# Windowed attention and a gated unit on one core: the gate's convolution in sixteen parts of the array, an added zero block, and a frozen order

## The chip, the core and the metric

The kernel runs on one core of a Trainium2 chip. The metric is the device time of one execution in microseconds. A core has five engines with a queue each: TensorE (PE, matrix products; its weight loads are shown apart as PEld), VectorE (DVE), ScalarE (ACT), GpSimd (POOL) and SyncE (SP, which here issues all transfers). Products go to PSUM, and DVE and ACT bring them back to SBUF.

## What is computed

Eight batches of 576 tokens, eight heads of 64. Heads 0 to 3 ("plain") look at the last 32 tokens, heads 4 to 7 ("dilated") at every fourth of the last 128. The attention result x, 512 wide, goes through a gated unit:

```python
scores = scale * np.matmul(q, k.transpose(0, 1, 3, 2))
mask_plain = (rel >= 0) & (rel < window)                    # window 32
mask_dil = (rel >= 0) & (rel < window * dilation) & (rel % dilation == 0)
attn = softmax(np.where(mask, scores, -1e9)); x = attn @ v
for k in range(K):                                          # K = 5, per channel
    gate_pre += conv_w[k][None, None, :] * xp[:, k:k + S, :]
gate = 1.0 / (1.0 + np.exp(-gate_pre))
val = x @ w_val
return (gate * val @ w_out)
```

## The kernel before

**Attention.** q and k come as fp32 into eight `qk` tiles; PE transposes their upper halves (read as bf16) into PSUM, and ACT or DVE copies them to `qT` and `kT`. Plain heads do this in groups of 18 transposes (`plain`, L581), dilated heads in groups of five (`dilated`, L647): four of 128 rows and one of the 64 rows that remain of 576. For each pair of heads, `attend` runs two score groups of six products (L513), exp on ACT (L520), the mask on DVE (L527), twelve products with v (L536), and the normalization on DVE (L545, L546). x is transposed back (L610 plain, L673 dilated) into `xT`, which holds 512 channels as four chunks of 128 partitions, for two batches side by side.

**The gated unit** (`gated`) works on two batches as three blocks of 384 tokens, the last two batches as four blocks of 288: 13 blocks. A block takes its four chunks in two pairs. For a pair the convolution (L716) is five taps of matmuls with a 64x64 diagonal matrix of the tap's weights as stationary operand, so a pair is 20 matmuls on 64x64 parts of the array, 26 groups in all. Then tanh on ACT (L727), the projection (L735, eight matmuls), and gate times value on DVE into `yT` (L745). In odd chunks the two halves of the channels change places in the convolution's output, and the weights are arranged to match. Last come 36 output tiles of 128 tokens (`outputs`: L765, copied out by L772 or L774, stored by L778).

**PSUM and buffers.** Three double tiles `pd` (two banks each; scores, products with v, plain transposes, convolution, projection) and two single tiles `pu` (dilated transposes, x transposes, outputs).

**What sets the order.** Each piece is a `Task` with the engines that may run it and estimated durations. `Plan.run` (L235) is a list scheduler: it keeps a clock for each engine, models the transfers and TensorE's clock, and at each step emits the task with the earliest start and best priority; the numbers in `TUNE` shift the priorities. It also inserts warm matmuls on a constant tile where it expects PE to wait (`emit`, L848 to L851). Each engine's queue runs in the order of emission. On SP at most five large loads are under way (`depth`), and a store waits in the same queue for its tile.

**Start.** `early` sets constants: the identity, masks, and the constant columns of the buffers. `weights` loads the convolution's weights (three small transfers, first in SP's queue now), builds `conv_diag`, loads `w_val` and `w_out` and casts them on POOL (w_val in 16 pieces of 64 columns, to set the channels in order).

Of the kernel before, what the change touches and what calls it, by code (L numbers as in the profile page):

```python
# [10 lines left out]
BF16 = mybir.dt.bfloat16  # L11
# [6 lines left out]
TUNE = {'seed': 918663,  # L18
 'jit': 0.211,
 'lag': 3.109,  # L20
 'plain': 0.758,
 'unit': -1.097,
 'half': -2.425,
 'chunk': 0.105,
 'look': {'PE': 0, 'ACT': 0.088, 'DVE': 0.03, 'POOL': 0.029, 'SP': 1.597},
 'flex': 0.555,
 'switch': 0.116,
 'conv': -3.876,
 'wv': 2.184,
 'wo': 0.85,  # L30
 'bufs': {'ps2': 3,
          'ps1': 2,
          'qk': 8,
          'vp': 2,
          'vd': 2,
          'vn': 2,
          'qT': 4,
          'kT': 4,
          'et': 5,
          'xn': 4,  # L40
          'gate': 3,
          'osb': 5,
          'xT': 3,
          'yT': 3,
          'vw': 2,
          'wt': 3},
 'kind': {'G': 1.939,
          'Xd': 1.011,
          'Ad': 0.718,
          'Sp': -5.15,  # L50
          'Tqp': 4.695,
          'Ap': 5.165,
          'Ekd': -5.633,
          'Eqd': 1.426,
          'ST': 2.599,
          'Y': -6.337,
          'Ed': -3.471,
          'Wv': -13.219,
          'Lqd': 0.336,
          'C': 0.77,  # L60
          'Lqp': 0.22,
          'Tqd': -0.449,
          'Lvp': 0.647,
          'Fp': 5.651,
          'U': 9.706,
          'H': 2.869,
          'Ep': -5.164,
          'Md': 1.158,
          'Ct': -1.059,
          'Xp': -1.728,  # L70
          'Tkd': 5.919,
          'Fd': -1.349,
          'Nd': -2.418,
          'Lc': -2.674,
          'Lwo': 2.488,
          'Sd': -3.39,
          'Wo': -6.282,
          'early': -0.684,
          'EO': 5.987,
          'Cd': 7.203,  # L80
          'Ekp': -10.843,
          'Tkp': -11.573,
          'Np': 3.065,
          'Lvd': 0.594,
          'Eqp': -4.056,
          'Lkr': -0.08,
          'Lkp': -0.622,
          'Mp': -3.736,
          'Lqr': -0.16,
          'Lwv': -0.381,  # L90
          'Lkd': 0.451,
          'V': 2.925,
          'O': 8.299,
          'HD': 8.634,
          'HA': -5.829,
          'HC': 11.348,
          'HB': 9.605,
          'Lvf': -0.397},
 'depth': 5,
 'heat': 6,  # L100
 'page0': 440,
 'lookq': 4.0,
 'nat': 4}
# [8 lines left out]
class Ten:  # L112


    def __init__(self, cls):
        self.cls = cls
        self.idx = None
        self.left = 0
        self.end = 0.0


class Task:
    def __init__(self, name, eng, fn, deps=(), tens=(), prio=0.0, mode=None, xfer=0.0, n=1, act=0.0, out=None):
# [5 lines left out]
        self.prio = prio  # L129
        self.mode = mode  # L130
        self.xfer = xfer
        self.n = n
        self.act = act
        self.out = out
        self.on = None
        self.load = False
        self.end = None
        self.users = []
        self.missing = len(self.deps)
        for d in self.deps:  # L140
            d.users.append(self)
        for t in self.tens:
            t.left += 1


class Plan:


    LAT = {PE: 0.22, ACT: 0.17, DVE: 0.17, POOL: 0.18, SP: 0.0}
    WIN, HOT, PAGE, FETCH = 3.4134, 0.40, 256, 1.1  # L150
    HEAT = 0.2133

    def __init__(self, counts):
        self.tasks = []
        self.free = {c: [0.0] * n for c, n in counts.items()}
        self.clock = {PE: 0.0, ACT: 0.0, DVE: 0.0, POOL: 0.0, SP: 0.0}
        self.mode = "128"
        self.dma = 0.0
        self.lanes = []
        self.loads = []  # L160
        self.landed = []
        self.log = []
        self.heats = 0
        self.act = {}
        self.slow = {}
        self.count = 0
        self.pages = {}
        self.bound = TUNE["page0"]
        self.rnd = random.Random(TUNE["seed"])

    def add(self, *a, **k):
        t = Task(*a, **k)
        kind = "".join(takewhile(str.isalpha, t.name))
        t.prio += TUNE["kind"].get(kind, 0.0) + self.rnd.uniform(-1.0, 1.0) * TUNE["jit"]
        self.tasks.append(t)
        return t
# [4 lines left out]
    def ready(self, t, eng):  # L181
        r = 0.0
        for d in t.deps:
            if d.on == SP or d.on == eng:
                e = d.end
            else:
                e = d.end + self.LAT[d.on]
            if e > r:
                r = e
        new = [x.cls for x in t.tens if x.idx is None]  # L190
        for c in set(new):
            e = sorted(self.free[c])[new.count(c) - 1]
            if e > r:
                r = e
        return r

    def speed(self, w):
        s = self.slow.get(w)
        if s is None:
            s = 2.0 if w < 1 or self.act.get(w - 1, 0.0) < self.HOT * self.WIN else 1.0  # L200
            self.slow[w] = s
        return s

    def pe_run(self, s, dur, act, n):
        t, i0 = s, self.count
        page = (i0 - self.bound) // self.PAGE + 1
        marks = []
        while self.bound + page * self.PAGE <= i0 + n:
            marks.append(((self.bound + page * self.PAGE - i0) / n, page))
            page += 1  # L210
        marks.append((1.0, None))
        done = 0.0
        for frac, p in marks:
            part = max(0.0, frac - done)
            while part > 1e-9:
                w = int(t / self.WIN)
                f = self.speed(w)
                end = (w + 1) * self.WIN
                need = part * dur * f
                step = min(need, end - t)  # L220
                if step < 1e-9:
                    step, end = min(need, self.WIN), end + self.WIN
                g = step / need * part
                self.act[w] = self.act.get(w, 0.0) + act * g
                t += step
                part -= g
            done = max(done, frac)
            if p is not None:
                t = max(t, self.pages.get(p, 0.0))
                wait = 1.1 + min(max(0.0, self.dma - t), TUNE["lookq"])  # L230
                self.pages[p + 1] = t + wait + self.FETCH
        self.count += n
        return t

    def run(self):  # L235
        cand = [t for t in self.tasks if t.missing == 0]
        n = len(self.tasks)
        INF = float("inf")
        self.loads.sort(key=lambda t: t.prio)
        depth = TUNE["depth"]  # L240
        look, flex, sw = TUNE["look"], TUNE["flex"], TUNE["switch"]
        while n:
            best = None
            for t in cand:
                if t.load and t is not self.loads[0]:
                    continue
                for eng, dur in t.eng.items():
                    s = max(self.clock[eng], self.ready(t, eng))
                    if s == INF:
                        continue  # L250
                    if eng == SP:
                        if len(self.lanes) >= 8:
                            s = max(s, self.lanes[-8])
                        if t.load and len(self.landed) >= depth:
                            s = max(s, self.landed[-depth].end)
                    at = max(s, self.clock[eng] + look[eng])
                    if eng == PE and t.mode != self.mode:
                        at += sw
                    if len(t.eng) > 1:
                        at += flex * dur  # L260
                    key = (at, t.prio, s + dur)
                    if best is None or key < best[0]:
                        best = (key, t, eng, dur, s)
            if best is None:
                raise RuntimeError("no task can go: " + ", ".join(t.name for t in cand[:20]))
            _, t, eng, dur, s = best
            cand.remove(t)
            n -= 1
            after = None
            if t.load:  # L270
                self.loads.pop(0)
                after = self.landed[-depth] if len(self.landed) >= depth else None
                if t.xfer > 0.5:
                    self.landed.append(t)
# [626 lines left out]
```

## Time and profile before

| | |
|---|---|
| runs | 179.76, 180.86, 181.28 us (median 180.86) |
| profiled execution | 180.61 us, its span 178.9 |
| PE busy | 159.3 us, 89% of the span |
| DVE, ACT, POOL busy | 68%, 62%, 19% |
| granted TensorE clock, mean | 0.968 |
| moved by DMA | 42.58 MB, mean 238 GB/s |
| largest parts of the chain that ended last | PE L765 16.5%, L735 14.2%, L716 9.6%, DMA of q 8.5%, L647 6.5% |

The span runs from the first to the last instruction; the execution's own time has 1.7 us around it. In the chain of waits a row is a start, a length, and what ran. In the groups by line, the two numbers behind the bar are the busy time of the group and the mean of one instruction in ns; what follows is the idle time of the engine just before, with what ended it. Busy time counts overlapping matmuls once, so it is less than count times mean. An array shape such as 64*64 stands with each matmul.

### The profile page before, as it was taken

The page shows a single profiled execution, that of the slowest core. Times are in us where ns is not written, and L with a number is a line of the kernel's source. Part 1 is how long each engine was busy: PE and PEld are TensorE (multiplying, and loading weights), DVE is VectorE, ACT ScalarE, POOL GpSimd, SP SyncE. Part 2 cuts the span into 40 slices and gives each one's busy share as a digit, 9 for nine tenths or more (in the row PEclk, how much of TensorE's full clock was granted, in tenths as well). Part 3 has the DMA queues.
Part 4 walks back from the last instruction along what each step waited for, and adds up shares of the span by engine and source line. Part 5 has one row for each costly group of instructions (what it writes and reads, how often), then busy time and mean ns, then how long its engine had stood idle before and what let it go on. Part 6 is the DMA issues. An engine that isn't in the chain of part 4 may idle for free.

```text
span 178.9 us, 5804 instructions
## 1 busy us (share of the span) xinstructions
PE 159.3 (89%) x2459; PEld 104.9 (59%) x2459; DVE 122.4 (68%) x242; ACT 110.8 (62%) x184; POOL 34.7 (19%) x64
## 2 busy tenths in 40 slices
PE   0888599897779998999998999999999999999990
PEld 0344475574566665665666676676656557776640
DVE  6524956977956876776899958599567928884210
ACT  2117598278784687768897282857668277544551
POOL 7003059556063201730030003020000000000000
PEclk9999859999879999999999999999999999999998
DMA  1899999999999999999999999997942143203334
GB/s 50 267 364 334 261 271 286 250 312 331 265 223 206 313 330 231 327 363 303 296 305 316 252 347 374 368 233 253 236 153 90 62 179 121 114 4 117 121 117 176
DMA packets 48385, 42.58 MB, mean 238 GB/s; under 512 B 23267, under 2 KB 38632, under 8 KB 48360
## 3 DMA queue, kind: packets, MB, share of 16 engines
q1 hardware_dynamic: 48360, 42.22, 82.1%
q8 instruction: 19, 0.31, 0.8%
q14 instruction: 6, 0.05, 0.1%
HBM read 32.78 MB, written 9.44 MB: 236 GB/s over the span
## 4 chain that ended last, share of the span: by engine, by line
PE 65%; DVE 12%; DMA 9%; ACT 8%; issue 3%; SPq 2%; ACTq 0%; DVEq 0%
PE pu L765 17%; PE pd L735 14%; PE pd L716 10%; DMA qk<-in_q_dram 9%; PE pu L647 7%; PE pd L536 5%; DVE xn L546 5%; PE pd L581 4%; ACT et L520 4%; PE pd L513 4%; DVE et L527 3%; PE pu L673 2%; PE pu L610 1%; PE pd L851 1%; ACT qT L492 1%
## 5 line engine op out<-in xcount | busy, mean ns | idle before, releaser
L520 ACT ACTIVATE et<-pd 128x576 bf16<-128x576 f32 x64 | 38.2, 654 | 9.6 <-PE pd L513 8.3
L527 DVE TENSOR_TENSOR et<-et,mask 128x576 bf16<-128x576 bf16 x64 | 31.6, 506 | 8.9 <-ACT et L520 6.7
L735 PE MATMUL pd<-xT,w_val 128*128 128x384 bf16 (+1 forms) x208 | 34.7, 313 | 0.9 <-DVE xn L546 0.9
L765 PE MATMUL pu<-w_out,yT 128*128 128x512 bf16 x144 | 34.8, 379 | 0.3 <-ACT kT L492 0.2
L772 ACT ACTIVATE osb<-pu 128x512 f32<-128x512 f32 x30 | 18.0, 600 | 27.2 <-PE pu L765 24.3
L546 DVE TENSOR_TENSOR xn<-pd,rec 96x768 bf16<-96x768 f32 x32 | 30.5, 954 | 1.1
L745 DVE SCALAR_TENSOR_TENSOR yT<-gate,pd 128x768 bf16<-128x768 bf16 (+1 forms) x26 | 23.1, 889 | 11.9 <-PE pd L735 11.8
L735 PEld LDWEIGHTS <-w_val 128*128 128x128 bf16 x208 | 19.0, 97 | 11.5 <-issue 1.8
L716 PE MATMUL pd<-xT,conv_diag 64*64 64x384 bf16 (+1 forms) x520 | 23.3, 320 | 0.0
L727 ACT ACTIVATE gate<-pd 128x768 bf16<-128x768 f32 (+1 forms) x26 | 19.5, 764 | 6.1 <-PE pd L716 5.6
L496 POOL CAST vn<-vd 128x1536 bf16<-128x1536 f32 x7 | 10.5, 1506 | 58.7 <-DMA vd<-in_v_dram 35.7
L513 PE MATMUL pd<-qT,kT 64*128 64x96 bf16 x384 | 15.4, 205 | 6.5 <-DVE xn L546 3.8
L765 PEld LDWEIGHTS <-yT 128*128 128x128 bf16 x144 | 12.9, 97 | 13.5 <-issue 0.7
L647 PE MATMUL pu<-ident,qk 128*128 128x128 bf16 (+1 forms) x160 | 17.9, 233 | 2.5 <-DMA qk<-in_q_dram 2.4
L513 PEld LDWEIGHTS <-kT 64*128 64x128 bf16 x384 | 10.1, 94 | 12.9 <-issue 10.2
L496 POOL CAST vw<-vp 32x384 bf16<-32x384 f32 (+2 forms) x27 | 13.7, 506 | 20.4 <-DMA vp<-in_v_dram 19.1
L716 PEld LDWEIGHTS <-conv_diag 64*64 64x64 bf16 x520 | 14.5, 108 | 5.1 <-issue 0.7
L647 PEld LDWEIGHTS <-qk 128*128 128x128 bf16 (+1 forms) x160 | 11.8, 103 | 9.3 <-DMA qk<-in_q_dram 3.4
L536 PEld LDWEIGHTS <-et 128*128 128x128 bf16 x384 | 14.8, 98 | 4.0 <-DVE et L527 0.6
L494 DVE COPY xT<-pu 128x576 bf16<-128x576 bf16 x19 | 11.2, 593 | 4.3 <-PE pu L610 4.3
L581 PE MATMUL pd<-ident,qk 128*64 128x128 bf16 x288 | 12.2, 244 | 0.0
L581 PEld LDWEIGHTS <-qk 128*64 128x64 bf16 x288 | 10.2, 125 | 3.4 <-issue 2.2
(53 smaller groups left out, 138.4 us busy)
## 6 DMA issues: line engine op xcount, KB each, us to landing
out_dram<-osb SPq DMA_DIRECT2D x36, 256.0 KB, 2.5
vd<-in_v_dram SPq DMA_DIRECT2D x8, 768.0 KB, 8.4
qk<-in_k_dram SPq DMA_DIRECT2D x8, 576.0 KB, 7.5
qk<-in_q_dram SPq DMA_DIRECT2D x8, 576.0 KB, 7.8
qk<-in_q_dram SPq DMA_DIRECT2D x8, 512.0 KB, 7.5
qk<-in_k_dram SPq DMA_DIRECT2D x8, 512.0 KB, 8.2
vp<-in_v_dram SPq DMA_DIRECT2D x4, 768.0 KB, 9.7
vp<-in_v_dram SPq DMA_DIRECT2D x4, 576.0 KB, 10.1
```

The source lines that it names most:

```text
L496: nc.gpsimd.tensor_copy(out_, in_)
L513: nc.tensor.matmul(out=ps2[ps.idx][:, l, QB * jj:QB * jj + QB], lhsT=kT[kt.idx][rb, c:c + 128], rhs=qT[qt.idx][rb, c:c + QB], start=True, ...
L520: nc.scalar.activation(out=et[e.idx][:, 0:2 * HW].rearrange("p (l n) -> p l n", l=2), in_=ps2[ps.idx][:, :, 0:HW], func=AF.Exp, scale=scale)
L527: (nc.vector if eng == DVE else nc.gpsimd).tensor_tensor(out=ev, in0=ev, in1=m, op=ALU.mult)
L536: nc.tensor.matmul(out=ps2[po.idx][:, hf, (2 * jj + l) * DA:(2 * jj + l + 1) * DA], lhsT=et[es[hf].idx][:, c:c + 128], rhs=val(j, l), star ...
L546: nc.vector.tensor_tensor(out=xn[xt.idx][0:QB].rearrange("p (h j) l d -> p h (j l) d", h=2), in0=a[:, :, :, 0:D], in1=rr[:, :, :, None].to ...
L581: nc.tensor.transpose(out=o[64 * y:64 * y + 64, 128 * j:128 * j + 128], in_=a[:, (y * PJ + j) * D:(y * PJ + j + 1) * D], identity=ident)
L647: nc.tensor.transpose(out=o[:, 128 * c:128 * c + m], in_=a[0:m, c * RD + 128 * cb:c * RD + 128 * cb + 128], identity=ident[0:m, 0:m])
L716: nc.tensor.matmul(out=dst(ps2[pc.idx][64 * ob:64 * ob + 64, n, 0:wd]), lhsT=conv_diag[rb, 2 * cp + n, kk, :], rhs=mov(2 * cp + n, rb, c0 ...
L735: nc.tensor.matmul(out=dst(ps2[pv.idx][:, n, 0:wd]), lhsT=w_val[:, mc, c * 128:(c + 1) * 128], rhs=mov(mc, slice(0, 128), c0), start=(mc = ...
L745: nc.vector.scalar_tensor_tensor(out=yT[yb.idx][:, 2 * cp:2 * cp + 2, t0:t0 + wd], in0=gate[gt.idx][:, :, 0:wd], scalar=1.0, in1=ps2[pv.id ...
L765: nc.tensor.matmul(out=ps1[po.idx], lhsT=yT[yb.idx][:, c, c0:c0 + 128], rhs=w_out[:, c, :], start=(c == 0), stop=(c == NCH - 1))
```

## The change

1. The convolution of a block is one group of 80 matmuls on all four chunks: diagonal matrices of 32x32, for each tap and chunk four row parts, part r of chunk n writing to column part r XOR n. It holds two `pd` tiles and two `gate` tiles (four for three) at once. `conv_diag` and `ident2` are half as wide.
2. The channels come out in another order, so the w_val cast has 24 pieces (8 of 64 and 16 of 32 columns), and w_out comes in eight transfers of 32 rows instead of four of 64.
3. The remainder of the dilated heads is transposed from all 128 rows; the lower 64 rows of that part of each `qk` tile are set to zero once, in `early`. The extra columns that come out are not read.
4. The scheduler and `TUNE` are gone. A string `ORDER` holds 731 words, each a task's number, its engine, and a count of warm matmuls ahead of it (28 in all; the scheduler put 15), and `HOMES` the buffer of each tensor. `run` only walks through it.

Besides the fewer convolution tasks, the string has another order of loads, of tasks on each engine, and another choice of ACT, DVE or POOL where several can do a task. The convolution's small loads stand behind ten other transfers.

```diff
-    def run(self):
-        cand = [t for t in self.tasks if t.missing == 0]
...
+        order = ORDER.split()
+        for word in order:
+            i = next(n for n, c in enumerate(word) if c.isalpha())
+            t, eng = self.tasks[int(word[:i])], self.ENG[word[i]]
+            t.heat = int(word[i + 1:] or 0)
...
+        for x in qk:
+            nc.vector.memset(x[64:128, 4 * RD:], 0.0)
...
                     for c in range(5):
-                        m = 128 if c < 4 else 64
-                        nc.tensor.transpose(out=o[:, 128 * c:128 * c + m],
-                                            in_=a[0:m, c * RD + 128 * cb:c * RD + 128 * cb + 128],
-                                            identity=ident[0:m, 0:m])
+                        nc.tensor.transpose(out=o[:, 128 * c:128 * c + 128],
+                                            in_=a[:, c * RD + 128 * cb:c * RD + 128 * cb + 128], identity=ident)
...
+            pcs, gts = [Ten("ps2") for _ in range(2)], [Ten("gate") for _ in range(2)]
+            def conv(eng, pcs=pcs, c0=c0, mov=mov, dst=dst, wd=wd):
+                for kk in range(K):
+                    for n in range(NCH):
+                        for r in range(4):
+                            ob = r ^ n
+                            rb = slice(G * r, G * r + G)
+                            nc.tensor.matmul(
+                                out=dst(ps2[pcs[n // 2].idx][G * ob:G * ob + G, n % 2, 0:wd]),
+                                lhsT=conv_diag[rb, n, kk, :], rhs=mov(n, rb, c0 + kk - (K - 1)),
+                                start=(kk == 0), stop=(kk == K - 1), tile_position=(G * r, G * ob))
...
-                def conv(eng, cp=cp, pc=pc, c0=c0, mov=mov, dst=dst, wd=wd):
-                    for kk in range(K):
-                        for n in range(2):
-                            for hb in range(2):
-                                ob = hb if n == 0 else 1 - hb
-                                rb = slice(64 * hb, 64 * hb + 64)
-                                nc.tensor.matmul(
-                                    out=dst(ps2[pc.idx][64 * ob:64 * ob + 64, n, 0:wd]),
-                                    lhsT=conv_diag[rb, 2 * cp + n, kk, :],
-                                    rhs=mov(2 * cp + n, rb, c0 + kk - (K - 1)),
-                                    start=(kk == 0), stop=(kk == K - 1))
...
-                for n, h in enumerate(VHEADS):
-                    copy(eng, w_val[:, 2 * pr:2 * pr + 2, n * D:(n + 1) * D], i[:, :, h * D:(h + 1) * D])
+                for to, frm, n in ((0, 0, 64), (64, 128, 64), (128, 96, 32), (160, 64, 32), (192, 224, 32), (224, 192, 32),
+                                   (256, 320, 64), (320, 256, 64),
+                                   (384, 480, 32), (416, 448, 32), (448, 416, 32), (480, 384, 32)):
+                    copy(eng, o[:, :, to:to + n], i[:, :, frm:frm + n])
...
+                for r, (a, b) in enumerate(parts):
+                    x = nc.sync.dma_start(
+                        out=wt[t.idx][G * r:G * r + G, :].rearrange("p (c n) -> p c n", c=2),
+                        in_=src_ap(moe_w_out, a * Dm, [[Dm, G], [(b - a) * Dm, 2], [1, Dm]]))
```

More of the change, by code (lines that the diff above doesn't have):

```diff
@@ L106, in hi_bf16 @@
+COUNTS = {'ps2': 3,
+ 'ps1': 2,
+ 'qk': 8,
+ 'vp': 2,
+ 'vd': 2,
+ 'vn': 2,
+ 'qT': 4,
+ 'kT': 4,
+ 'et': 5,
+ 'xn': 4,
+ 'gate': 4,
+ 'osb': 5,
+ 'xT': 3,
+ 'yT': 3,
+ 'vw': 2,
+ 'wt': 3}
+DEPTH = 5
+NAT = 4
 def hi_bf16(ap: bass.AP) -> bass.AP:
@@ L128, in __init__ @@
         self.tens = [t for t in tens if t is not None]
[L129 to L133, printed above, removed]
[L134 to L143 removed]
+        self.out = out
+        self.load = load
+        self.big = big
+        self.heat = 0
+        self.after = None
+        self.done = False
 class Plan:
[L149 to L153, printed above, removed]
+    ENG = {"P": PE, "A": ACT, "V": DVE, "G": POOL, "S": SP}
+    def __init__(self):
         self.tasks = []
[L155 to L169, printed above, removed]
     def add(self, *a, **k):
         t = Task(*a, **k)
[L173 to L174 removed]
         self.tasks.append(t)
@@ L179, in emit @@
         t.fn(eng)
[L181 to L233, printed above, removed]
```

427 lines of the change are left out of this document (151 added, 276 removed).

## The prediction

> **What bounds the kernel now.** I read the page's first part, then busy time by stage, then the chain that ended last, then the groups by shape.
>
> ```profile
> span 178.9 us, 5804 instructions
> PE 159.3 (89%) x2459; PEld 104.9 (59%) x2459; DVE 122.4 (68%) x242; ACT 110.8 (62%) x184; POOL 34.7 (19%) x64
> ```
> ```profile
> 0.00:20.00 20.00, 12.00 (x131) 6.75 (x133) 10.25 (x46) 6.77 (x10) 4.73 (x13) 1.00 0.84 259
> 20.00:60.00 40.00, 34.92 (x626) 24.76 (x625) 30.28 (x55) 29.52 (x50) 19.04 (x38) 0.87 1.09 265
> 60.00:100.00 40.00, 38.02 (x605) 24.82 (x606) 32.31 (x57) 29.63 (x50) 8.01 (x11) 1.00 1.06 306
> 100.00:122.00 22.00, 22.00 (x367) 14.79 (x364) 16.84 (x30) 12.62 (x21) 2.94 (x2) 1.00 1.06 319
> 122.00:140.00 18.00, 17.69 (x282) 11.65 (x277) 13.26 (x27) 13.23 (x22) 0.00 (x0) 1.00 0.58 167
> 140.00:160.00 20.00, 19.95 (x308) 13.43 (x307) 14.54 (x24) 10.79 (x19) 0.00 (x0) 1.00 0.28 107
> ```
>
> The columns after the stage are its length, then busy time (instructions) of PE, PEld, DVE, ACT, POOL, the granted clock, the DMA share and GB/s. From 60 us to 160 us PE is busy 97.7 of 100 us; no other engine is over 81%. Before 60 us PE idles 13.1 us, while the DMA engines are full (0.84, then 1.09). So there are two limits, one after the other: the loads at first, TensorE later. The chain shows the seam:
>
> ```profile
> 59.41 9.06 DMA qk<-in_q_dram
> 68.52 0.99 PE pu L647 x10
> ...
> 84.47 0.23 PE pd L513 x6
> 84.70 1.75 PE pd L716 x40
> 86.46 0.23 PE pd L513 x6
> 86.69 0.46 PE pu L647 x5
> 87.15 0.48 PE pd L536 x12
> 87.63 0.36 PE pu L647 x5
> ...
> 88.82 0.13 PE pd L513 x6
> ...
> 89.92 0.62 PE pd L581 x18
> ...
> 99.35 0.38 PE pd L536 x12
> 99.73 1.30 PE pd L735 x8
> ...
> 138.09 0.86 PE pu L765 x4
> ...
> 155.18 1.40 PE pd L716 x40
> ...
> 157.66 0.38 PE pd L536 x12
> ```
>
> At 68.5 us the transposes of batch 4 (L647 x10) start as their 9.06 us load lands; from there to the end the chain is mostly PE, so PE work removed behind 68.5 us is time, and PE work removed ahead of it is mostly waiting for loads. That seam carries the forecast.
>
> **The convolution.** L716 makes 26 groups of 20 matmuls on 64x64 parts, four at once: first-to-last, two groups take 1.75 us at 384 columns and 1.40 us at 288. How close is that to four at once?
>
> ```profile
> 84.63 0.68 PE L716 MATMUL pd<-xT,conv_diag 64*64 64x384 bf16 x12
> ```
> ```profile
> 84.63 0.85 PE L716 MATMUL pd<-xT,conv_diag 64*64 64x384 bf16 x16
> ```
> ```profile
> L716 PE MATMUL pd<-xT,conv_diag 64*64 64x384 bf16 x360 | 17.6, 335 | 0.0
> L716 PEld LDWEIGHTS <-conv_diag 64*64 64x64 bf16 x520 | 14.5, 108 | 5.1 <-issue 0.7
> L513 PEld LDWEIGHTS <-kT 64*128 64x128 bf16 x384 | 10.1, 94 | 12.9 <-issue 10.2
> ```
>
> The first 12 matmuls of a group cover 0.68 us and the first 16 cover 0.85: four more, of 335 ns each, add 0.17 us. L735 streams 384 columns in 1.30/8 = 0.163 us. So a wave of four takes the time of one stream, and weights are changed under it at no cost. The new block puts all 16 matmuls of a tap in one wave, so 80 matmuls take five streams where a pair of groups took ten. A pair less its entry change of shape (0.10, below) is 1.65 and 1.30 us; a block's stream is 0.825 and 0.65, plus the later start of 12 more parts. The nearest row for that start is a weight load's own time, 14.5/520 = 28 ns, as an upper end (0.33 us, once a block); the lower end is 0. Four matmuls fitting in 0.17 us lies nearer to 0, so I take 0.04.
>
> **Changes of array shape.** L513's group of six takes 0.23 us behind another shape (84.47, 86.46) and 0.13 behind a 64-row transpose, its own shape (88.82); L536's 12 take 0.48 behind L513 and 0.38 otherwise. A change costs 0.10 us. Counted in the two written orders there are 149 before and 134 after, 83 and 78 of them behind the first transpose of batch 4. The remainder's two changes go, but the new order alternates scores with other work more often and hands much of that back.
>
> **The transposed remainder.**
>
> ```profile
> L647 PE MATMUL pu<-ident,qk 128*128 128x128 bf16 x128 | 14.1, 239 | 2.5 <-DMA qk<-in_q_dram 2.4
> L647 PE MATMUL pu<-ident,qk 64*128 64x64 bf16 x32 | 6.6, 207 | 0.0
> ```
>
> Own time of a remainder is 6.6/32 = 0.206 us with its change, of a full one 14.1/128 = 0.110 at most. Five take 0.36 with one change: (0.36 - 0.10)/4.5 = 0.058 for a full one, half for the remainder. Streaming all 128 rows adds 0.029 each; the changes are counted above.
>
> **Behind the seam, task by task in the written orders.** Convolution: before 11 groups at 384 and 8 at 288, 11 x 0.825 + 8 x 0.65 = 14.3; after 6 and 4 blocks, 6 x 0.865 + 4 x 0.69 = 7.95; gain 6.3. Output tiles (L765, 0.86): 35 before, 33 after; gain 1.7. L581's 18 transposes (0.62): 5 before, 4 after; gain 0.6. Score groups (0.13): 36 and 35; 0.1. Remainders: 16 x 0.029 = 0.5 lost. Changes: 5 x 0.10 = 0.5. The projection L735 and the products L536 are the same in number. Sum 8.7 us.
>
> **The start.**
>
> ```profile
> 0.80 0.70 SPq L794 DMA_DIRECT2D osb<-in_moe_conv_w_dram  x2
> ...
> 1.88 0.56 SPq L465 DMA_DIRECT2D qk<-in_k_dram  x1
> ...
> 123.05 0.45 SPq L482 DMA_DIRECT2D vp<-in_v_dram  x1
> ```
> ```profile
> L851 PE MATMUL pd<-warm 128*128 128x512 bf16 x11 | 4.3, 510 | 0.2 <-ACT et L520 0.2
> L851 PE MATMUL pu<-warm 128*128 128x512 bf16 x4 | 1.8, 496 | 0.0
> L496 POOL CAST w_val<-wt 128x128 bf16<-128x128 f32 x16 | 5.2, 371 | 0.3 <-DMA wt<-in_moe_w_val_dram 0.2
> L411 DVE MEMSET warm<- 128x256 uint32 x1 | 0.3, 272 | 0.9 <-PEq L885 0.9
> ```
>
> The small convolution loads, first on SP now, move behind ten others: the first large load goes at 0.8 and not 1.88, 1.1 us sooner, and up to the seam the same bytes are ahead of batch 4's q (v for the plain heads of batch 3 in place of k of batch 4). Gain 1.1. Eight memsets of qk come in (nearest row 272 ns, 2.2 us on DVE before its first transposed tile): the fourth load waits for the third memset, about 3.2 us by the listed memsets against 2.5 us when SP reaches it, and holds the queue behind it 0.7 us while three loads fly; 0, or 0.7 if they are done. Warm matmuls go from 15 to 28, 13 x 0.41 = 5.3 us at the measured own time, all but two of the 28 ahead of the first convolution, in the stage where PE idles 13.1 us; 0, at worst 5.3. The w_val cast has 24 pieces for 16, 16 of them half as wide: between 0 and 8 x 371 ns = 3.0 us on a POOL busy 19%, hidden unless the first projection waits for it. w_out comes in 8 DMAs for 4: four more issues of about 0.5 us in a queue that runs ahead; 0, and 2 us if the load stream were short of issues.
>
> **New waits.** A block takes two of the three double PSUM tiles at once where a group took one.
>
> ```profile
> L727 ACT ACTIVATE gate<-pd 128x768 bf16<-128x768 f32 x18 | 14.6, 812 | 5.7 <-PE pd L716 5.4
> L545 DVE RECIPROCAL rec<-pd 96x12 f32<-96x12 f32 x32 | 7.1, 222 | 4.7 <-PE pd L536 4.4
> L546 DVE TENSOR_TENSOR xn<-pd,rec 96x768 bf16<-96x768 f32 x32 | 30.5, 954 | 1.1
> ```
>
> The longest holder is the normalization, 0.222 + 0.954 = 1.18 us. In the written order work that uses no double tile stands between, or work on the third: for example transposes, L536 and a projection, some 2.6 us, between two blocks of the same pair of batches. Between 0 and 1.18 per block over ten blocks; the listed cover is longer than the holder, so I take 0.1 each: 1.0. Instructions of PE go from 4913 to 5979; the chain of the page gives 3% (5.4 us) to issue, and if all of it were PE's supply and grew by 22% it would be 1.2: I take 0.5. The stores are interleaved sooner, 21 before the last load for 15: 6 x 256 KB at 0.319 MB per us is 4.9 us later for it. Now it is issued at 123.05 and L536 of batch 7 uses it at 157.66, so 4.9 us fit in; 0.
>
> Sum on the span: 178.9 - 8.7 - 1.1 + 1.0 + 0.5 = 170.6. The profiled execution took 180.61, 1.7 more than its span, and the median of three is 180.86. Predicted: 170.6 + 1.7 = 172.
>
> **The rivals.** *No more at once than now*: 32-row parts stream side by side only as far as 64-row ones do, so a block takes as long as the pair. Then 6.3 is lost: 178.6, at the edge of what a measurement of this kernel tells from no change (1%). Nothing here shows 16 parts; against it, four parts show no loss. 0.08.
>
> *Weight loads set the pace* (slower): 80 loads of 28 ns one after another are 2.23 us a block. Behind the seam that is 10 x 2.23 - 7.95 = 14.4 more: 186. It evens out the gain from 0.89 us above my block, about 21 ns a load. For: L513's loads also own 10.1/384 = 26 ns. Against: those loads wait for nothing scarce, and narrower ones should take less. 0.07.
>
> *PSUM* (slower): each of 10 blocks waits the full 1.18 us: 172 + 10.8 = 183. It turns at 0.99 a block. 0.07.
>
> *Row groups exclude each other*: a weight load waits until the matmul in its own rows is done, so in each row group the chunks go one by one, 20 streams a block, 3.26 us at 384. Behind the seam: 6 x 3.26 + 4 x 2.60 = 30 for 7.95, 194. By that a group of today would need 10 x 0.163 = 1.63 us, and it takes 0.88: 0.02. [...] The trace of this kernel does not agree, since parts of the same rows ran together at 0.17 us a wave. [...]
>
> *The seam moves too*: the order shortens the first 68 us by more than the 1.1, at most by the work removed there, 13.1 us of idle with a 0.87 clock being what could be won; some 5 us gives 167. 0.06.
>
> **How the numbers follow.** My own case has 0.70, its range 168 to 177 (from all new waits nil and half of the last rival's gain to half the upper ends of the waits). Range of all: 166 to 180, which leaves out the last three slower cases and the far end of the others, 0.2. Faster by over 1% (below 179): 0.70 + 0.06 + half of 0.08 = 0.80. Within: the other half and a little of PSUM, 0.05. Slower: 0.15.
>
> **What would show it.** Right: a block of 80 matmuls first-to-last near 0.9 us with its entry, five waves 0.16 apart; no 64x64 form under the dilated transposes; PE over 95% busy from 70 us on. Wrong: matmuls of one tap spread over 0.3 us; PE waiting for tanh or normalization ahead of the blocks; batch 4's transposes later than 68 us; PE idle before batch 7's scores, waiting for a DMA.

## The result, and the profile after

The changed kernel takes 179.59 us (median of 12 executions, 176.94 to 183.52) against 181.19 us for the kernel before (12 executions, 179.76 to 184.18). The ratio is 0.9867, 95% interval 0.9818 to 0.9916: 1.3% faster, where the prediction had 172 us, 5% faster. Executions of one kernel fall into a faster and a slower state, and the ratios here and below compare the faster ones alone, so this one differs from that of the two medians (0.991). The direction was right; 172 was too low by 7.6 us, of which the traces below place some seven. The profiled execution of after took 178.58 us, its span is 176.9.

First the page of after, its first part and its instruction queue (packets, MB, share of the 16 DMA engines), then the same queue in the page of before:

```profile
span 176.9 us, 6853 instructions
PE 154.8 (88%) x2992; PEld 99.3 (56%) x2992; DVE 123.1 (70%) x254; ACT 103.2 (58%) x174; POOL 41.6 (24%) x80
q8 instruction: 23, 0.38, 0.9%
```
```profile
q8 instruction: 19, 0.31, 0.8%
```

PE is busy 4.5 us less than before (154.8 for 159.3), but the span is only 2.0 us shorter. So PE has less to do and is idle more. Busy time by stage, after, with the columns of the prediction's table, says where:

```profile
20.00:60.00 40.00, 34.19 (x753) 23.79 (x751) 30.69 (x56) 28.88 (x49) 19.72 (x44) 0.96 1.04 272
60.00:100.00 40.00, 36.42 (x778) 24.27 (x777) 31.72 (x58) 27.39 (x48) 10.22 (x14) 1.00 0.98 304
100.00:122.00 22.00, 22.00 (x393) 14.07 (x391) 17.75 (x32) 14.20 (x25) 1.32 (x1) 1.00 0.87 270
122.00:140.00 18.00, 14.96 (x271) 9.20 (x267) 11.67 (x23) 9.68 (x17) 1.50 (x1) 0.91 0.56 157
140.00:160.00 20.00, 20.00 (x453) 12.78 (x450) 15.58 (x27) 10.59 (x18) 0.00 (x0) 1.00 0.44 120
```

Behind the seam, where the prediction wanted PE over 95% busy, two stages fall out: from 60 to 100 us PE is busy 1.6 us less than before (36.42 for 38.02), and from 122 to 140 us 2.7 less (14.96 for 17.69), there with a granted clock of 0.91. The chain of after names what stood there:

```profile
62.51 9.16 DMA qk<-in_k_dram
71.72 0.45 PE pu L465 x5
...
91.56 1.10 PE pd L530 x80
...
95.48 0.81 PE pd L530 x52
96.28 2.07 issue
98.35 0.54 PE pd L530 x28
...
129.25 1.10 PE pd L530 x80
130.34 0.59 PE pd L550 x3
130.94 3.00 issue
133.94 3.97 PE pd L550 x13
...
148.40 0.98 PE pd L530 x80
```

L530 is the convolution, L550 the projection, L465 the dilated transposes. Two pieces are called issue: PE stands for 2.07 us in the middle of a convolution block, after 52 of its 80 matmuls, and for 3.00 us three matmuls into a projection. No semaphore released either of them. Behind the second, 13 projection matmuls take 3.97 us; at the 0.163 us of before they would take 2.12.

The seam and the end, in the timeline of after (the number in brackets is idle time, with what ended it), and the end of before:

```profile
67.42 0.45 PE L465 MATMUL pu<-ident,qk 128*128 128x128 bf16 x5 [0.42 <-DMA qk<-in_q_dram]
...
168.55 4.51 PE L579 MATMUL pu<-w_out,yT 128*128 128x512 bf16 x20
```
```profile
170.15 4.52 PE L765 MATMUL pu<-w_out,yT 128*128 128x512 bf16 x20
```

The first transposes of batch 4 came 1.10 us sooner (67.42 for 68.52); a last wait for a load, of k, follows at 71.72, with 0.52 us of idle time, and the chain of after runs through that load. From the first transposes to the last matmul before takes 170.15 + 4.52 - 68.52 = 106.15 us and after 168.55 + 4.51 - 67.42 = 105.64: 0.5 us gained, where the prediction's sum has 8.7 - 1.0 - 0.5 = 7.2. In this stretch PE is busy 99.70 us for 104.73, and idle 5.87 us for 1.37. So the missing time lies behind the seam.

### The profile page after: what moved, and what is told of

The parts are those of the page before. It is cut to its first block, busy times and chain, and to the rows that moved or that the text cites. A ratio compares the mean times of both kernels' runs of the same rounds, so it can differ in the third digit from the quotient of the medians.

```text
span 176.9 us, 6853 instructions
## 1 busy us (share of the span) xinstructions
PE 154.8 (88%) x2992; PEld 99.3 (56%) x2992; DVE 123.1 (70%) x254; ACT 103.2 (58%) x174; POOL 41.6 (24%) x80
## 4 chain that ended last, share of the span: by engine, by line
PE 66%; DMA 18%; DVE 8%; issue 4%; ACT 1%; SPq 0%; ACTq 0%; DVEq 0%
PE pd L550 19%; PE pu L579 17%; DMA qk<-in_k_dram 14%; PE pd L530 8%; PE pd L358 5%; PE pd L335 4%; PE pu L465 4%; PE pd L403 4%; DMA qk<-in_q_dram 3%; PE pu L489 3%; PE pu L430 2%; DVE et L349 2%; DVE xn L368 2%; DVE xT L316 1%; DVE qT L316 1%
## 5 line engine op out<-in xcount | busy, mean ns | idle before, releaser
L550 PE MATMUL pd<-xT,w_val 128*128 128x384 bf16 (+1 forms) x208 | 37.1, 323 | 3.4 <-issue 3.0
L579 PE MATMUL pu<-w_out,yT 128*128 128x512 bf16 x144 | 36.4, 380 | 0.0
L550 PEld LDWEIGHTS <-w_val 128*128 128x128 bf16 x208 | 19.5, 99 | 15.5 <-issue 5.9
L318 POOL CAST vn<-vd 128x1536 bf16<-128x1536 f32 x8 | 12.0, 1497 | 62.2 <-DMA vd<-in_v_dram 56.4
L586 ACT ACTIVATE osb<-pu 128x512 f32<-128x512 f32 x27 | 16.2, 598 | 16.8 <-PE pu L579 12.1
L318 POOL CAST vw<-vp 32x384 bf16<-32x384 f32 (+2 forms) x34 | 17.6, 519 | 17.7 <-DMA vp<-in_v_dram 16.2
L465 PE MATMUL pu<-ident,qk 128*128 128x128 bf16 x160 | 14.7, 226 | 5.8 <-DMA qk<-in_k_dram 4.1
L530 PE MATMUL pd<-xT,conv_diag 32*32 32x384 bf16 (+1 forms) x1040 | 15.4, 314 | 2.4 <-issue 2.1
L358 PEld LDWEIGHTS <-et 128*128 128x128 bf16 x384 | 15.0, 97 | 4.3 <-issue 1.2
L465 PEld LDWEIGHTS <-qk 128*128 128x128 bf16 x160 | 10.2, 101 | 10.2 <-DMA qk<-in_k_dram 3.9
L530 PEld LDWEIGHTS <-conv_diag 32*32 32x32 bf16 x1040 | 10.6, 88 | 7.5 <-issue 5.8
L314 ACT COPY qT<-pd 128x576 bf16<-128x576 bf16 x11 | 6.8, 646 | 8.8 <-PE pd L403 8.8
```

Of the source, the lines that this page charges most:

```text
L318: nc.gpsimd.tensor_copy(out_, in_)
L358: nc.tensor.matmul(out=ps2[po.idx][:, hf, (2 * jj + l) * DA:(2 * jj + l + 1) * DA], lhsT=et[es[hf].idx][:, c:c + 128], rhs=val(j, l), star ...
L465: nc.tensor.transpose(out=o[:, 128 * c:128 * c + 128], in_=a[:, c * RD + 128 * cb:c * RD + 128 * cb + 128], identity=ident)
L530: nc.tensor.matmul(out=dst(ps2[pcs[n // 2].idx][G * ob:G * ob + G, n % 2, 0:wd]), lhsT=conv_diag[rb, n, kk, :], rhs=mov(n, rb, c0 + kk - ( ...
L550: nc.tensor.matmul(out=dst(ps2[pv.idx][:, n, 0:wd]), lhsT=w_val[:, mc, c * 128:(c + 1) * 128], rhs=mov(mc, slice(0, 128), c0), start=(mc = ...
L579: nc.tensor.matmul(out=ps1[po.idx], lhsT=yT[yb.idx][:, c, c0:c0 + 128], rhs=w_out[:, c, :], start=(c == 0), stop=(c == NCH - 1))
```

## Where the stalls come from

**Each lies 256 instructions, or a multiple, from the others.** Counted in the written order of PE's instructions (a weight load and its matmul count as two), PE stops ahead of number 3255 at 96.28 us and ahead of 4535 at 130.94 us; a shorter stop, 1.29 us at 55.53, lies at 1719. These are 6 x 256 and 5 x 256 apart. (From the start of the last instruction before a stop to the start of the next one the three are 1.5, 2.4 and 3.3 us, as the expectations of e1 and e2 have them.) The page of the profile has 0.38 MB in 23 packets in the instruction queue, some 16 KB each, and before had 19 for 4913 PE instructions where after has 23 for 5979: four packets more for 1066 instructions, again some 256 a packet. By these counts PE's program arrives in pages of 256 instructions while the kernel runs: in after the 23 transfers of that queue begin between 20.30 and 165.44 us. Worked out from the trace's transfer records, for some pages (us):

```text
                 page entered   fetch of the next   next entered
before, 3255     116.12         120.25 - 121.59     124.17
after, 1463       51.72          54.53 -  55.41      56.82  (stall 1.29)
after, 2999       92.03          95.97 -  97.12      98.35  (stall 2.07)
after, 4279      126.53         131.49 - 132.47     133.94  (stall 3.00)
after, 4791      141.29         143.20 - 144.16     148.66
after, 5559      160.01         160.04 - 161.26     164.26
```

At the three stalls the fetch begins 2.8, 3.9 and 5.0 us after the page before it was entered, takes about 1.0 us, and PE goes on 1.2 to 1.5 us after it lands. These three pages lasted 5.1, 6.3 and 7.4 us with the stops behind them, and hold 3.8 to 4.4 us of work. From the entry of the page to the start of that fetch the DMA share was 1.01, 1.10 and 0.91. Late in the kernel, where the DMA engines have less to move (their share is 0.44 from 140 to 160 us and 0.48 from 160 to 176), the fetch begins within 2 us in the two rows above, and nothing waits. Before issues a page in 5.3 to 10 us and has no such stop. After, a page is worked off in as little as 4.3 us while the loads run (the one entered at 87.77 us, whose next fetch begins 1.1 us later, and nothing waits): a block is 160 instructions in 1.1 us. My theory became: the gain of the convolution is real, and the supply of instructions takes it back, because the change runs 22% more instructions in less time while the loads fill the DMA engines (shares 1.04 and 0.98 in the two stages from 20 to 100 us). The rival: the 32x32 form itself makes PE stop (weights exchanged under running matmuls of the same rows), and its place by number is chance.

## The experiments

All times are medians; ratios are to the kernel before, measured beside it, with 95% intervals. "64x64 form" is the convolution on 64x64 parts, in the changed kernel's order, buffers and remainder; its wider diagonals are built beside the narrow ones (14 more DVE instructions).

**e1_conv64: the old shape in the new order.** A block is 40 matmuls again; PE has 4939 instructions. In short (the run has the new loops in a second function beside the old one):

```diff
-                    for n in range(NCH):
-                        for r in range(4):
-                            ob = r ^ n
-                            rb = slice(G * r, G * r + G)
+                    for n in (0, 2, 1, 3):
+                        for hb in range(2):
+                            ob = hb ^ (n // 2)
+                            rb = slice(64 * hb, 64 * hb + 64)
```

> The block's convolution goes back to 64x64 parts (40 matmuls in ten streams for 80 in five); order, buffers and all else as in the changed kernel, whose profiled execution took 178.6 us. Supply theory: TensorE stood 1.5, 2.4 and 3.3 us at instructions 1719, 3255 and 4535, each 256 apart from an earlier fetch of 16 KB, until the fetch had landed, and the half clock after the last one cost 1.9 more. With 4939 instructions for 5979 a page lasts a fifth longer, so these waits go (about 8 us back), and ten blocks behind the first 68 us cost 6 x 0.65 + 4 x 0.39 = 5.5 more: about 176. Rival, the loads and the order set the end and the stalls only stand where other waits would: 5.5 more, 184.

Measured: 178.13 us, ratio 0.9796 (0.9701 to 0.9891). One block (one of its 40 records is missing), and the instruction queue:

```profile
135.78 1.75 PE pd L548 x39
```
```profile
q8 instruction: 19, 0.31, 0.8%
```

No piece over 0.5 us of its chain behind the seam is called issue. The time is nearer to the theory's 176 us than to the rival's 184. The rest of the change (order, buffers, remainder) is worth about 2%, and with a convolution that takes 1.75 us a block, not 1.10, the kernel is no slower than after. Used in every block, as in after, the new shape shows no gain in the end, though each block is 0.65 us shorter.

**e2_depth3: fewer loads under way.** At most three large loads fly, not five.

```diff
-DEPTH = 5
+DEPTH = 3
```

> At most three large loads under way instead of five; nothing else. Supply theory: the fetches at 96.0 and 131.5 us began 3.9 and 4.9 us after TensorE had entered the page before, behind loads in the DMA engines; with three fifths of the loads ahead they begin about 2 to 3 us after it, the stalls of 2.4 and 3.3 us fall below 1.5 each, and the time to 174 to 177 unless the load stream itself slows. Rival, the loads set the pace up to 72 us: fewer under way means a later batch 4, 180 to 186.

Measured: 179.24 us, 0.9871 (0.9791 to 0.9951). PE's longest waits:

```profile
PE pd L358 <- POOL vn L318: 3.7, 3, 2.5
PE pu L465 <- DMA qk<-in_k_dram: 3.4, 4, 1.6
PE pd L550 <- issue: 2.7, 1, 2.7
PE pd L530 <- issue: 2.3, 2, 1.4
```

This missed. The waits named issue stay, the fetches still begin up to 4.5 us after the page before was entered, and the products with v (L358) now wait longest, for the casts of v on POOL. The number of large loads under way is not what delays the fetch, or three are still enough.

**e3_shift128: the page borders moved.** 64 tiny warm matmuls at the start, 128 instructions, while PE has nothing else to do.

```diff
+        if t.name == "early":
+            for _ in range(64):
+                nc.tensor.matmul(out=ps1[0][:, 0:8], lhsT=warm[:, 0:128], rhs=warm[:, 0:8], start=True, stop=True)
```

> 64 small warm products (128 instructions of TensorE, 8 columns each) at the very start, where TensorE waits for the first load: every page boundary falls 128 instructions sooner in the order, nothing else moves. Supply theory: the three stalls leave their places (first tile transposes behind block 2, the middle of block 5, the first projection of block 7); pages that now last under some 5 us are those from about 88 to 98 us and 133 to 142 us, so smaller stalls appear there: 174 to 178. Rivals (width of the block, loads, PSUM): no effect, 179.6.

Measured: 176.87 us, 0.9785 (0.9709 to 0.9861). The longest pieces of its chain that are called issue:

```profile
61.24 1.18 issue
...
75.17 1.35 issue
...
95.81 1.02 issue
...
101.68 1.35 issue
```

More work on PE, and a lower median than after's, though the intervals of the two ratios overlap: the two long stops left their places, there is none near 130 us any more, and those that came elsewhere are shorter. The same instructions with the same operands no longer stop, so it isn't what they do that stops them. Counted in each kernel's own instructions, every stop of over 0.2 us that is called issue in after, e2, e3 and e8 lies a multiple of 256 from the others. The gain is not a cure; it depends on where the borders fall.

**e8_rows_outer: another sequence within a tap.** The sixteen matmuls of a tap go by rows, then chunks; the count stays.

```diff
-                    for n in range(NCH):
-                        for r in range(4):
+                    for r in range(4):
+                        for n in range(NCH):
```

> The changed kernel with the two inner loops of a tap swapped, so that four matmuls in a row use the same 32 rows instead of four different row parts. Measured so far: a block takes 1.10 us at 384 columns and 0.98 at 288 first to next, and weight load and matmul of a part follow each other every 8 ns. If that pace is the issue of instructions, the block stays at 1.10 and 0.98. If loads into the same rows queue (row groups exclude each other), it gets longer, 1.3 or more. If row parts now collide less, 0.97.

Measured in one execution: 178.66 us. From its chain:

```profile
94.97 0.81 PE pd L530 x50
95.78 2.52 issue
98.30 0.54 PE pd L530 x28
...
129.25 1.10 PE pd L530 x80
130.94 3.13 issue
```

A block still takes 1.10 us, and both long stops are there, the first before the same 28 remaining matmuls (two records of the 52 are missing). The sequence of row and column parts in a tap matters neither to the block nor to the stops.

**e9_split64: as many instructions, the old shape.** e1 with each matmul cut into two column halves, 80 a block. PE then has 5979 instructions, as after; the array works on 64x64 tiles.

```diff
+                for h in range(2):
...
-                                out=dst(ps2[pcs[n // 2].idx][64 * ob:64 * ob + 64, n % 2, 0:wd]),
-                                lhsT=conv_diag64[rb, n, kk, :], rhs=mov(n, rb, c0 + kk - (K - 1)),
+                                out=o[cut], lhsT=conv_diag64[rb, n, kk, :], rhs=i[cut],
```

> The 64x64 convolution in the changed kernel's order, as in e1_conv64, but each matmul cut into two column halves: 80 matmuls a block as in the changed kernel, so its instruction pages begin at the same places, while the array works on the tile pairs of e1. If the supply of instructions is what cost the changed kernel its gain, the waits named issue of 2 to 3 us come back (the changed kernel had 1.5, 2.1 and 3.0) and the time is 3 to 7 us above e1's 178.1: 181 to 185 us. If the 32x32 form itself makes the stalls, there are none here and the time is e1's plus the cost of shorter matmuls, 178 to 180 us.

Measured: 182.85 us, 1.0098 (1.0041 to 1.0155), by medians 4.7 us above e1; the intervals of the two ratios lie apart. Its chain:

```profile
96.67 1.20 PE pd L553 x52
97.87 1.19 issue
99.06 0.78 PE pd L553 x24
...
130.72 1.79 PE pd L553 x80
132.51 0.59 PE pd L573 x3
133.10 2.84 issue
135.94 4.34 PE pd L573 x13
```

With no 32x32 matmul in it, the kernel stops at the same two instructions as after: in the middle of the one block, and three projections behind the other, with the same 13 slow matmuls behind it (four records of the first block are missing; counted by weight loads the places are the same). In this execution the stops and the slow matmuls are 1.19 + 2.84 + (4.34 - 2.12) = 6.3 us, and ten blocks behind the seam at 1.79 for 1.75 are 0.4. That can't be set against the 4.7 us between the medians piece by piece: the profiled execution of e9, 184.26 us, is 1.4 above its median, and that of e1, 176.07, is 2.1 below its own. That both stops come back decides between the two: it is the number of instructions, not the form.

**e4_mixed, e7_mixed3, e6_mixed4: the new shape where the loads are light.** The 64x64 form early, the 32x32 form in the last four blocks (e4), also in two blocks of the third pair of batches (e7), or in all three of them and one of the pair before (e6): 5259, 5419 and 5579 PE instructions.

```diff
+            if (g, k) not in ((1, 0), (2, 0), (2, 1), (2, 2)) and g < 3:
+                conv = conv_64
```

(e6; e7 names only (2, 0) and (2, 2), e4 has only the last condition.)

> 64x64 parts in the nine blocks of the first six batches, 32x32 parts in the last four blocks, which run after 148 us when few loads are left. 5259 instructions. Supply theory: as with 64x64 throughout, without the 4 x 0.39 us of the last blocks: about 174.5. Rival, the loads and the order: 6 x 0.65 = 3.9 more than the changed kernel, 183.

> As the mixed kernel, but blocks 0 and 2 of pair 2 are in 32x32 parts too; 5419 instructions. Supply theory: 2 x 0.65 less, 174.2 for 175.5. Rival as above: 176.

> As the mixed kernel, but blocks 0 of pair 1 and all of pair 2 are in 32x32 parts too; 5579 instructions, only blocks 1 and 2 of pair 1 (which stand 4 us apart) and the three of pair 0 are 64x64. Supply theory: in the mixed kernel the pages of these blocks left 4 to 7 us between the landing of the next page and its entry, more than the 1.3 us that every stalled page shows, so four blocks gain 0.65 each: 173 for 175.5. Rival, any block in sixteen parts while loads run costs a stall: 176 to 178.

Measured: e4 175.47 us, 0.9680 (0.9626 to 0.9734); e7 174.54, 0.9697 (0.9594 to 0.9800); e6 174.22, 0.9687 (0.9617 to 0.9756). All three beat both kernels, and none of their chains has a piece called issue of over 0.4 us behind the seam. e4 and e1 were measured side by side: 174.80 to 175.65 us for e4 and 176.07 to 178.84 for e1, so the new shape in the last four blocks gains some 2 us (0.9680 for 0.9796), where 4 x 0.39 = 1.6 was worked out. Among themselves the three can't be told apart: what two or four more blocks in the new shape were to add (174.2 and 173 us were expected) isn't shown.

**e5_rem128: the remainder alone, in the old kernel.** The scheduler, order and convolution of before, with only the zeroed rows and the transposes from 128 rows.

```diff
+        for x in qk:
+            nc.vector.memset(x[64:128, 4 * RD:], 0.0)
...
-                                            in_=a[0:m, c * RD + 128 * cb:c * RD + 128 * cb + 128],
-                                            identity=ident[0:m, 0:m])
+                                            in_=a[:, c * RD + 128 * cb:c * RD + 128 * cb + 128], identity=ident)
```

> The kernel before, with nothing but the remainder transposed from 128 rows (and its zero block); scheduler, order and the 64x64 convolution stay. Behind the first transposes of batch 4 the order then has 57 changes of array shape for 83; at 0.10 us each 2.6 us go, 16 remainders of 0.029 us come back: 2.1 us faster, about 179 where the kernel before takes 181. Rival, a change of shape hides beside the copies that the transposes feed: same time as before.

Measured: 181.0 us, 1.0001 (0.9958 to 1.0043), the rival's time and not the 179 expected, though not for the rival's reason. Its first long wait of PE, and its seam:

```profile
PE pu L804 <- DVE ident_f L438: 6.2, 1, 6.2
```
```profile
70.37 0.73 PE L648 MATMUL pu<-ident,qk 128*128 128x128 bf16 x10 [0.65 <-DMA qk<-in_q_dram]
```

Ten transposes take 0.73 us for the 0.99 of before: 0.13 us won for each remainder; two changes of shape less the longer stream would be 0.17. But L804, PE's wait for DVE at the start, was 4.1 us before and is 6.2 now: the eight memsets, 2.2 us, stand ahead of it, and the seam lies at 70.37 us, 1.85 later. From the seam to the last matmul e5 takes 105.02 us and before 106.16: 1.1 us are won there, where 2.1 were expected, and the start gives them back in that order.

**e10_rem64 beside e6, e12_rem64 beside e11_mixed4: the remainder from 64 rows again, in the mixed kernel.** e11 is the kernel of e6 again.

```diff
-        for x in qk:
-            nc.vector.memset(x[64:128, 4 * RD:], 0.0)
...
+                        m = 128 if c < 4 else 64
```

> e6_mixed4 with the dilated remainder transposed from 64 rows again and without the zeroed rows (eight memsets less). If changes of the tile shape on TensorE cost what the prediction took, 104 against 78 of them behind the seam at 0.10 us less 0.5 us for the shorter transposes make it 2.1 us slower than e6_mixed4: about 176.3 us against 174.2. If they are hidden or given back at the start, as e5_rem128 had it in the old order, it takes the same 174.2 us.

> The kernel of e6_mixed4 once more, beside the next on the same chip. Ratio to the kernel before as there, 0.962 to 0.976, about 174.5 us.

> The kernel of e10_rem64 once more, on the same chip as e11_mixed4. If each change of the tile shape costs 0.10 us behind the seam, 1 to 2 us above e11_mixed4; if the gain is given back at the start of the kernel, within 0.5 us of it.

Measured: e10 175.91 us, 0.9667 (0.9580 to 0.9754), no difference from e6, which was measured on the same chip at another time (0.9687). Side by side: e11 173.18 us (172.57 to 173.83, six executions; ratio 0.9663, 0.9566 to 0.9760), e12 175.20 (174.20 to 177.22, six; 0.9764, 0.9655 to 0.9873): 2.0 us apart and the executions don't overlap, though the intervals of the two ratios do. For e10 it had been worked out as 2.1, all of it behind the seam. The traces don't bear out that place. The two profiled executions are 2.9 us apart. From the first transposes of batch 4 to the last matmul e12's takes 101.28 us and e11's 100.18, so 1.1 us are won there, as in e5 and in e6 against e10 (100.33 and 101.41). The other 1.8 us came ahead of the seam (66.89 for 68.69), where the sum had nothing. So the total agrees with 2.1 in part by luck. PE's busy time in that stretch is 1.8 us less in e5 than before, 1.7 less in e11 than in e12 and 0.6 less in e6 than in e10; in the first two pairs other waits took part of it back. So 0.10 us for a change of shape isn't confirmed as a price in time: half of what was worked out from it shows. The zeroed rows pay where the start has room for their memsets. Groups of transposes in e12, then in e11:

```profile
L472 PE MATMUL pu<-ident,qk 128*128 128x128 bf16 x128 | 13.8, 236 | 2.3 <-DMA qk<-in_k_dram 2.3
L472 PE MATMUL pu<-ident,qk 64*128 64x64 bf16 x32 | 6.5, 204 | 1.4 <-DMA qk<-in_k_dram 1.4
```
```profile
L473 PE MATMUL pu<-ident,qk 128*128 128x128 bf16 x160 | 15.0, 231 | 3.9 <-DMA qk<-in_k_dram 3.6 <-DVE xT L324 0.3
```

The same 160 transposes take 15.0 us busy for 20.3.

The lowest ratio of the study is that of e11's kernel, 0.966 of before. Its chain shows what is left:

```profile
61.83 8.80 DMA qk<-in_k_dram
...
123.26 7.75 DMA qk<-in_q_dram
...
133.92 1.10 PE pd L538 x80
...
143.26 0.58 issue
...
154.05 0.98 PE pd L538 x80
```

A load of q, issued at 123 us, is now on the chain behind the seam, and PE waits 0.21 us for it at 131.05: PE has come near the loads again, and less work on it ahead of that would probably be a longer wait. The 0.58 us of issue lie at a page border too, so the mixed kernel isn't wholly free of such stops.

## Why the prediction was wrong

**The step that failed: "if all of it were PE's supply and grew by 22% it would be 1.2: I take 0.5".** It scaled an existing, unrelated share with the number of instructions (of the 5.4 us, the pieces of the chain add up to 4.5). The supply isn't a rate; it is a limit, page by page, that the pages of before, 5.3 to 10 us long, never met. Behind the seam it cost 2.07 + 3.00 us of stops and 3.97 - 2.12 = 1.85 us of slow matmuls, 6.9 us for 0.5. The stop of 1.29 us ahead of the seam probably cost nothing, since at 67.42 PE waits for a load anyway; no run took it out alone. The profile of before had no wait that could show this; what it had was the instruction queue's 19 packets, from which the pages could have been worked out. The prediction also read the idle time of PE before 60 us as waiting for loads. From 20 to 60 us that was wrong, though the sum didn't use it: there the long waits of PE in the trace of before end with DVE (some 4 us) and ACT (1.1 us), none with a load.

**Also off, the size of a block.** Predicted 0.865 and 0.69 us with an entry of 0.10, measured 1.10 and 0.98. That is 0.135 x 6 + 0.19 x 4 = 1.6 us behind the seam. The trace's single starts show why: the first tap's sixteen start within 50 ns, 3 ns apart, but from the third tap on they start 8 ns apart, so the last tap's sixteen spread over 136 ns, and taps follow at 0.176 us for 0.165. My 0.04 for the late start of twelve parts should have been about 0.1. In the 64x64 form (e1, and L716 of before at 84.63 us) the four of a wave start within 10 ns to the end.

**Against them, the wait for PSUM** never came: 1.0 us was set aside, and no wait of a convolution for tanh or the normalization shows. Together 6.4 + 1.6 - 1.0 = 7.0 us; missing behind the seam were 6.7. The smaller terms (output tiles, transposes, changes of shape) aren't tested one by one; L581's groups of 18 behind the seam are 9 and 8 in the traces, not 5 and 4, which leaves the gain of one group as it was.

**Right.** The sixteen parts do run at once, five waves to a block, so three rivals fell, which had 1.75 us a block (no more at once than now), 2.23 (weight loads as the pace; the 1040 loads of 32x32 are busy 10.6 us in all, 10 ns each and not 28) and 3.26 (row groups that exclude each other) for the 1.10 measured. The seam stayed at batch 4 and came 1.10 us sooner, so the rival by which it moves five us fell too. That this is the 1.1 of the start to the digit is luck: e8, with the same loads and tasks, has the same transposes at 66.56. A change of shape at 0.10 us isn't confirmed: of the 2.1 us worked out with it, 1.1 show behind the seam in each pair of e5, e10 and e12; in this sum it weighs little, with five changes. The warm matmuls and the casts of w_val cost the changed kernel nothing that shows. The chain of after does run through three of the memsets of qk into a load of q, which goes at 3.15 us in after and e11 and at 2.44 in e12, without the memsets. But the transposes that wait for it start at 8.74 us in e11 and at 9.05 in e12, so the prediction's 0 fits; in the old order the memsets cost 2.1 us at the start (e5). The time of 179.6 lies in the range, at its upper end, by a mechanism that was a term of half a microsecond and should have been a rival.

**Shown and open.** That the number of instructions and not the 32x32 form makes the stops is shown by e9 and e1, that their place goes with the count by e3, that the shape's gain is real where they are absent by e4 beside e1. What makes a fetch begin as late as 5.0 us after the page before was entered is not settled: the late ones lie where loads are under way, though not every fetch there is late, and three loads instead of five didn't shorten it. A page border placed on purpose between loads wasn't tried.

## What to carry to other kernels

Price the instructions that a change adds to TensorE by the stretch where they run: divide its instructions there by 256, the page of these traces, and ask whether 256 of them still last until the next page is there under that stretch's DMA load, here 5 to 7.5 us at the pages that stopped. In this kernel the form that does the same work in twice the instructions belonged where the loads are done, and the shorter program where they are not; the mixes gave 3.0 to 3.4% where the new form throughout gave 1.3% and the old form in the new order 2.0%. Read a piece named issue of over a microsecond, in the middle of one unbroken group, as a question about the instruction queue, and shift the count once to see if it moves.

## What the runs showed that I had not expected

PE's granted clock fell after the stop of 3.0 us. Two windows of after, the stop and what follows; then those of e2, whose stop was 2.67 us, and one of e9, behind its stop of 2.84 us (the granted clock stands third from the end):

```profile
130.90:134.00 3.10, 0.10 (x2) 0.06 (x2) 0.06 (x1) 0.93 (x2) 1.39 (x1) 1.00 0.61 225
134.00:138.00 4.00, 4.00 (x19) 1.77 (x21) 0.95 (x1) 0.00 (x0) 0.00 (x0) 0.57 0.03 7
```
```profile
132.30:134.90 2.60, 0.00 (x0) 0.00 (x0) 0.00 (x0) 0.87 (x2) 1.47 (x1) 1.00 0.74 274
135.00:137.00 2.00, 2.00 (x13) 1.12 (x13) 0.95 (x1) 0.00 (x0) 0.00 (x0) 1.00 0.04 11
```
```profile
136.00:140.00 4.00, 4.00 (x13) 1.69 (x13) 0.95 (x1) 0.00 (x0) 0.00 (x0) 0.50 0.02 4
```

After 3.00 us the clock was 0.57 on the mean of 4 us, after 2.84 us (e9) 0.50, after 3.13 us (e8) 0.50 from 136 to 138 us, and after 2.67 us it stayed at 1.00. The length of the stop is not the whole of it: in before the clock was 0.50 from 48.07 to 51.48 us, and the longest wait of PE in the 3.41 us ahead of that was 0.81 us. In the clock records of these traces the clock changes at times that lie 3.41 us apart, or a multiple of that: in after it is 0.50 from 134.36 to 137.77 us, in e9 from 135.05 to 141.88. In the 3.41 us ahead of the fall PE was still busy for 0.42 us in after and for 1.46 in e9. Where these stretches lie in e2, continued from its last change at 51.41 us, the stop is split between two of them, with PE busy 2.36 and 1.79 us. That it depends on where in them a stop falls is my estimate from these figures, not shown, and the busy time of one stretch doesn't settle it: PE was busy 2.25 us in the one ahead of the fall in before, and 1.87 us in that from 96.81 to 100.22 us in after, behind which the clock stayed at 1.00. The stop of 3.00 us, with its 1.85 us of slow matmuls, cost 1.6 times its own length.
